# First MoE in five chunks of 480 or 384 tokens instead of eight of 288, with new due times for the list

## The chip, the cores and the metric

The kernel runs on one core of a Trainium2 chip. The metric is device time in microseconds of one execution, as the median of several runs; lower is better. The core has five engines that work through queues of their own, each in order: TensorE (PE) for matmuls, VectorE (DVE), ScalarE (ACT), GpSimd (POOL), and SyncE (SP), whose queue here issues all DMAs. Work on different engines is ordered by semaphores alone. SBUF is the on-chip memory, PSUM the eight banks that matmuls write.

## What is computed

```python
def _attn_ref(q, k, v):            # 4 batches, 8 heads, 576 tokens, 64 per head
    ...
    masks = np.stack([mask_plain if h < H // 2 else mask_dil for h in range(H)], axis=0)
    scores = np.where(masks[None, :, :, :], scores, -1000000000.0)
    ...
    return np.matmul(attn, v).astype(np.float32)

def _moe_ref(x, w1, w2, w3, w_out):    # 2304 tokens, 512 -> 1024 -> 512
    a = x @ w1
    b = x @ w2
    h = a * b @ w3
    return (h @ w_out).astype(np.float32)

def _moe2_ref(x, w_in, w_out, a, b):   # 2304 tokens, 512 -> 2048 -> 512
    h = x @ w_in
    ...
    g = P / (Q + 1e-06)
    return (g @ w_out).astype(np.float32)
```

Windowed attention (in half of the heads over every fourth token), then a first MoE block, then a second with a rational function in its middle. The weights arrive as float64.

## The kernel before

The kernel multiplies W3 by Wout once (`w3_mm`, W3o), so that the first MoE is two layers: x @ w1 and x @ w2 with their product (L1), then the product @ W3o (L2). Every operand of these layers is split into a high and a low part of type float32r, and a product is three matmuls: high by high, high by low, low by high. A weight slab arrives as 64-bit words and is turned into float32 by ACT and DVE: `scale` on ACT, then `shift`, `sign`, `low_bits` on DVE; or, for the slabs that the constants BY_ACT name, `top_bits` on ACT as well and only `ends` and `middle` on DVE. Then `high` on ACT and `low` on DVE split it.

Work comes in two stages. In the first (`phase1`, to 437.9 us) nothing is issued where it is written. All of it, attention by batch, pair of heads and half (G from 0 to 31), W3o, the 16 slabs of w1 and w2, both layers by chunk, and the preparation of the second MoE's 32 slabs that goes back to DRAM as `wd`, is given to a planner (`Plan`) as jobs with an engine, an estimated duration, predecessors, buffers and a due time. The planner plays the engines through and takes, on each engine, the ready job of the earliest due time; the instructions are then issued in the order of the starts that it found. That order is fixed from then on: on the chip an engine waits for the head of its queue. Due times come from the table T, which `main_jobs` fills in the order W3o, L1 and L2 of each chunk, and from constants (GAP, AHEAD, LEAD, B_FROM, PACE).

The tokens of the first MoE are cut into eight chunks of TA = 288, two for a batch of 576. `l1(k, m, e)` is a group of 12 matmuls into one of the two banks `ab`; ACT copies the first of a pair (`l1_copy`, tile a_sb), DVE multiplies it by the second (`l1_mul`, tile p), ACT and POOL split the product (`l1_high`, `l1_low`, tile pp). Chunk 0 and 1 run their first layers together, slab by slab; the products of chunk 1 are stored to DRAM and loaded again (`p_store`, `p_load`) since SBUF doesn't hold both. `l2(k, h, i)` accumulates the second layer in two banks for each half h, `acc` and then `ab` (in the last chunk `sc`); ACT and DVE split the result (x2, x2l) and SP stores it as `x2d`.

The attention output of a batch is one tile xs in pool xs01 (batches 0 and 2, on the right side of SBUF) or xs23 (1 and 3, on the left). The words of the second MoE's slabs go through two buffers in turn, w32 and w33. Each of these slabs is one turn: load, `scale`, three steps on DVE, store to `wd`, and the buffer is free for the next load.

The second stage (`phase2`) runs the second MoE over token blocks of 512 (the last of 256), with x loaded back from x2d as tiles XS0 to XS4 (XS0, XS1 and XS4 in pool b3 on the right, XS2 and XS3 in b1 on the left). It begins with one step, then runs L2 of the last chunk (`tail`) and goes on.

Of the kernel before, what the change touches and what calls it, by code (L numbers as in the profile page):

```python
# [26 lines left out]
TA = 288  # L27
NA = NT // TA
# [159 lines left out]
class Kern:  # L188
# [277 lines left out]
    def l1_copy(self, k, m):  # L466
        self.a_sb[k, m] = self.tp.tile([P, TA], F32, tag="t", bufs=5, name="a_sb")
        self.nc.scalar.copy(self.a_sb[k, m], self.ab[k, m, 0][:, 0:TA])

    def l1_mul(self, k, m):  # L470
        p = self.pp[k, m] = self.tp.tile([P, TA], F32, tag="t", bufs=5, name="p")
        self.nc.vector.tensor_tensor(out=p, in0=self.a_sb[k, m], in1=self.ab[k, m, 1][:, 0:TA],  # L472
                                     op=ALU.mult)

    def l1_high(self, k, m):
        p, e = self.pp[k, m], m % 2
        if e == 0:
            self.p2[k, m // 2] = self.gp.tile([P, 2, 2, TA], F32R, tag="g", bufs=5, name="pp")
        self.nc.scalar.copy(self.p2[k, m // 2][:, 0, e], p)  # L479
# [589 lines left out]
```

## Time and profile before

| what | us |
|---|---|
| median of 3 runs | 854.42 |
| lowest and highest run | 854.24, 855.56 |
| span of the profiled execution (first to last instruction) | 852.4 |
| first stage, to the first matmul of the second MoE (L848) | 437.9 |
| PE busy | 840.8 |
| DVE, ACT, POOL busy | 569.0, 546.2, 328.5 |

The page gives no time of its own for the profiled execution beside its span; the span stands 2.0 us under the median. Busy times say how long an engine had an instruction in work; for PE the ends of matmuls are modelled and neighbours overlap, so the distance of starts is the better measure. Lines such as L462 are lines of the kernel before; in the changed kernel the same work has other line numbers (L462 becomes L487, L513 becomes L522, L225 becomes L229).

### The profile page before, as it was taken

The numbers are of one execution on the slowest core, as the hardware profiler recorded it, in microseconds if no ns is written. First come the engines' busy times: TensorE is split into PE (matmuls) and PEld (weight loads), VectorE is DVE, ScalarE is ACT, GpSimd is POOL, SyncE is SP. The second block draws the span as 40 slices with busy tenths as digits, with TensorE's granted clock in tenths as the row PEclk, the third lists the DMA queues.
The fourth block names the chain that finished last, engine by engine and source line by source line (L and its number), as shares of the span: only waits on it lengthen the run. The fifth ranks groups of instructions, "written<-read, shape, count | busy, mean of one in ns | idle before, by whom it ended". The sixth has DMA issues, their size and how long they took to land.

```text
span 852.4 us, 14597 instructions
## 1 busy us (share of the span) xinstructions
PE 840.8 (99%) x5256; PEld 722.5 (85%) x5256; DVE 569.0 (67%) x1240; ACT 546.2 (64%) x1226; POOL 328.5 (39%) x305
## 2 busy tenths in 40 slices
PE   9999999999999999999999999999999999999998
PEld 5557789989999999999998788888888888888886
DVE  6999985777657223411226887788778777797775
ACT  7787677664466335622336977777777777777773
POOL 1330123223043212402124665565556655564443
PEclk9999999999999999999999999999999999999999
DMA  9986275875866212070343000010000100001112
GB/s 352 321 315 216 88 252 188 276 252 177 282 200 212 71 48 76 2 253 1 106 141 125 13 13 25 13 37 26 13 13 25 37 14 14 13 25 50 42 42 90
DMA packets 43464, 95.06 MB, mean 112 GB/s; under 512 B 4736, under 2 KB 13952, under 8 KB 43392
## 3 DMA queue, kind: packets, MB, share of 16 engines
q1 hardware_dynamic: 43392, 94.13, 32.6%
q8 instruction: 41, 0.67, 0.3%
q14 instruction: 31, 0.25, 0.1%
HBM read 71.57 MB, written 22.54 MB: 110 GB/s over the span
## 4 chain that ended last, share of the span: by engine, by line
PE 89%; ACT 5%; DMA 3%; DVE 2%; issue 0%; POOL 0%; SPq 0%; POOLq 0%; DVEq 0%; ACTq 0%
PE ab L462 24%; PE acc L898 11%; PE sc L898 11%; PE ab L848 11%; PE px L848 10%; PE acc L513 6%; PE ab L513 4%; PE sc L351 2%; PE acc L442 2%; PE px L409 2%; PE px L394 2%; PE ab L442 1%; ACT pr L375 1%; PE sc L442 1%; PE px L307 1%; PE sc L513 1%
## 5 line engine op out<-in xcount | busy, mean ns | idle before, releaser
L462 PE MATMUL ab<-xs,w 128*128 128x288 f32 x1536 | 215.9, 299 | 2.6 <-DVE x2l L526 2.2
L462 PEld LDWEIGHTS ab<-xs,w 128*128 128x128 f32 x1536 | 205.7, 188 | 8.4 <-DVE x2l L526 2.9
L859 POOL TENSOR_TENSOR y<-y,v 128x512 f32<-128x512 f32 x72 | 95.9, 1331 | 142.9 <-ACT y L858 142.6
L387 POOL TENSOR_TENSOR pr<-pr,sm 96x384 f32<-96x384 f32 x64 | 57.6, 919 | 173.3 <-DVE sm L382 98.4
L898 PE MATMUL acc<-w,gg 128*128 128x512 f32 x432 | 109.8, 391 | 1.5 <-ACT r L869 1.5
L898 PE MATMUL sc<-w,gg 128*128 128x512 f32 x432 | 109.4, 391 | 0.0
L483 POOL TENSOR_TENSOR pp<-p,pp 128x288 fp32r<-128x288 f32 x56 | 47.2, 843 | 158.5 <-ACT pp L479 158.4
L848 PE MATMUL ab<-XS,w 128*128 128x512 f32 (+1 forms) x480 | 105.4, 370 | 0.0
L848 PE MATMUL px<-XS,w 128*128 128x512 f32 (+1 forms) x480 | 105.3, 370 | 0.0
L885 POOL TENSOR_TENSOR gg<-t,gg 128x512 fp32r<-128x512 f32 x72 | 93.7, 1302 | 10.6 <-ACT gg L884 10.1
L848 PEld LDWEIGHTS px<-XS,w 128*128 128x128 f32 x480 | 83.9, 188 | 16.3
L848 PEld LDWEIGHTS ab<-XS,w 128*128 128x128 f32 x480 | 83.8, 188 | 16.2
L898 PEld LDWEIGHTS acc<-w,gg 128*128 128x128 f32 x432 | 80.8, 188 | 19.2 <-ACT r L869 1.9
L898 PEld LDWEIGHTS sc<-w,gg 128*128 128x128 f32 x432 | 80.9, 188 | 17.2
L472 DVE TENSOR_TENSOR p<-a_sb,ab 128x288 f32<-128x288 f32 x64 | 29.0, 453 | 85.3 <-PE ab L462 67.0
L375 ACT ACTIVATE pr<-pr,sm 96x128 f32<-96x128 f32 x192 | 74.7, 393 | 2.5 <-DVE sm L367 2.5
L876 DVE SCALAR_TENSOR_TENSOR v<-y,cs,r 128x512 f32<-128x512 f32 x72 | 71.3, 990 | 0.0
L868 ACT ACTIVATE r<-y,cs 128x512 f32<-128x512 f32 x72 | 52.3, 726 | 14.5 <-POOL y L859 14.4
L479 ACT CAST pp<-p 128x288 fp32r<-128x288 f32 x56 | 24.2, 432 | 56.5 <-DVE p L472 56.5
L858 ACT ACTIVATE y<-v,cs 128x512 f32<-128x512 f32 x72 | 58.8, 817 | 2.4
L225 ACT ACTIVATE dec<-words 128x512 f32<-128x512 f32 x72 | 47.5, 672 | 19.3 <-DMA words<-moe_w_in 8.4
L513 PE MATMUL acc<-pp,w 128*128 128x288 f32 x384 | 55.1, 298 | 0.0
(90 smaller groups left out, 1298.1 us busy)
## 6 DMA issues: line engine op xcount, KB each, us to landing
words<-moe_w SPq DMA_DIRECT2D x32, 512.0 KB, 6.2
words<-moe_w_out SPq DMA_DIRECT2D x24, 512.0 KB, 4.4
words<-moe_w_in SPq DMA_DIRECT2D x16, 512.0 KB, 4.4
wd<-dec SPq DMA_DIRECT2D x32, 256.0 KB, 2.3
c<-wd SPq DMA_DIRECT2D x32, 256.0 KB, 2.6
vb<-v SPq DMA_DIRECT2D x16, 384.0 KB, 4.2
XS<-x2d SPq DMA_DIRECT2D x6, 1024.0 KB, 6.9
kT<-k SPq DMA_DIRECT2D x16, 304.0 KB, 4.3
```

The source lines that it names most:

```text
L225: self.nc.scalar.activation(out=d.bitcast(F32), in_=s["words"].bitcast(F32)[:, :, 1], func=AF.Copy, scale=2.0 ** -112)
L375: self.nc.scalar.activation(out=pr[:, i], in_=pr[:, i], func=AF.Exp, scale=-1.0, bias=sm[:, 0, i:i + 1], accum_out=sm[:, 1, i:i + 1])
L387: self.nc.gpsimd.tensor_tensor(out=pr[:, i], in0=pr[:, i], op=ALU.mult, in1=sm[:, 2, i].unsqueeze(2).to_broadcast([QT, 3, P]))
L462: self.nc.tensor.matmul(t[:, 0:TA], w[:, s[0], c * P:(c + 1) * P], xs[:, s[1], c, tok], start=n == 0, stop=n == 11)
L513: self.nc.tensor.matmul(self.l2_acc[k, n][:, 0:TA], self.W3o[m][0][:, a, n * P:(n + 1) * P], self.p2[k, i][:, c, m % 2], start=m == 0 and ...
L848: nc.tensor.matmul(t[:, e * nt:(e + 1) * nt], w[:, s[0], c * P:(c + 1) * P], XS[blk][:, s[1], c], start=n == 0, stop=n == 11)
L858: nc.scalar.activation(out=w, in_=v, func=AF.Identity, scale=self.b1, bias=self.b0)
L859: nc.gpsimd.tensor_tensor(out=w, in0=w, in1=v, op=ALU.mult)
L868: nc.scalar.activation(out=r, in_=yy[i][1], func=AF.Ln, bias=self.c1)
L876: nc.vector.scalar_tensor_tensor(out=v, in0=w, scalar=self.c1, in1=r, op0=ALU.add, op1=ALU.mult)
L885: nc.gpsimd.tensor_tensor(out=t[:, 1], in0=u, in1=t[:, 0].bitcast(F32), op=ALU.subtract)
L898: nc.tensor.matmul(acc[g, blk][tk], t[:, s[0], j:j + P], w[:, s[1]], start=f + e == 0 and s == (0, 0), stop=f + e == FG - 1 and s == (1, 0))
```

## The change

The first MoE is cut into five chunks of 480, 480, 384, 480 and 480 tokens (CH) that cross the batches. Each chunk has an xs tile of its own, in three slots: chunks 0, 2 and 3 in pool xsa on the right, 1 and 4 in xsb on the left. The output of one half of a pair of heads may lie in two chunks and is then written in two pieces. Chunk 1 no longer runs with chunk 0: the list's order is W3o in full, then L1 and L2 chunk by chunk; all products stay in SBUF (tile g: eight buffers of 2 x 512), and the DRAM tile pd with its stores and loads is gone. The W3 slabs rotate through five buffers instead of six, the second MoE's slabs all through w32. Four W3 slabs and eight of w1 and w2 are done by ACT's top_bits instead of eight and sixteen. Due times (GAP0, GAP, AHEAD0, AHEAD, PACE, W3_AT) and the planner's durations are set anew.

```diff
-TA = 288
-NA = NT // TA
+CH = ((0, 480), (480, 480), (960, 384), (1344, 480), (1824, 480))
+NA = len(CH)
+TM = max(n for _, n in CH)
+NR = 3
+HS = S // 2
...
-TL = NT - TA - BLK[NB - 2][0]
+TL = CH[-1][0] - BLK[NB - 2][0]
...
-W12SLOT = ("p0", "p1", "p2", "p3", "w34", "w35", "w30", "w31",
+NW3 = 5
+W12SLOT = ("p0", "p1", "p2", "p3", "w33", "w34", "w30", "w31",
...
-GAP0, GAP = 4.0, 7.0
+GAP0, GAP = 3.0, 9.0
...
-W3_AT = 4
-PACE = 1.15
-
-BY_ACT3 = 8
-BY_ACT1, BY_ACT2 = 0, 16
+AHEAD0, AHEAD = 14.0, 16.0
+W3_AT = 8
+PACE = 1.25
+
+BY_ACT3 = 4
+BY_ACT1, BY_ACT2 = 0, 8
...
     def att_high(self, G):
-        b = G // (2 * HP)
-        if b not in self.xs:
-            pool = (self.xs01, self.xs23)[b % 2]
-            self.xs[b] = pool.tile([P, 2, KC, S], F32R, tag="xs", bufs=1, name="xs")
-        dst, src = self.att_x(G)
-        self.nc.scalar.copy(dst[:, 0], src)
+        for c in self.fresh.get(G, ()):
+            pool = (self.xsa, self.xsb, self.xsa)[c % NR]
+            self.xs[c] = pool.tile([P, 2, KC, CH[c][1]], F32R, tag=f"xs{c % NR}", bufs=1, name="xs")
+        for dst, src in self.att_x(G):
+            self.nc.scalar.copy(dst[:, 0], src)
 
     def att_low(self, G):
-        dst, src = self.att_x(G)
-        self.nc.vector.tensor_tensor(out=dst[:, 1], in0=src, in1=dst[:, 0].bitcast(F32),
-                                     op=ALU.subtract)
+        for dst, src in self.att_x(G):
+            self.nc.vector.tensor_tensor(out=dst[:, 1], in0=src, in1=dst[:, 0].bitcast(F32),
+                                         op=ALU.subtract)
...
     def l1(self, k, m, e):
-        xs, w, tok = self.xs[k // 2], self.w12[2 * m + e]["w"], slice(k % 2 * TA, (k % 2 + 1) * TA)
+        xs, w, nt = self.xs[k], self.w12[2 * m + e]["w"], CH[k][1]
...
-                self.nc.tensor.matmul(t[:, 0:TA], w[:, s[0], c * P:(c + 1) * P], xs[:, s[1], c, tok],
+                self.nc.tensor.matmul(t[:, 0:nt], w[:, s[0], c * P:(c + 1) * P], xs[:, s[1], c],
...
-    def p_store(self, m):
-        self.nc.sync.dma_start(out=self.pd[m // 2, :, m % 2], in_=self.pp[1, m])
-
-    def p_load(self, i):
-        w = self.p2[1, i] = self.gp.tile([P, 2, 2, TA], F32R, tag="g", bufs=5, name="pp")
-        self.nc.sync.dma_start(out=w[:, 1].bitcast(F32), in_=self.pd[i])
...
-                self.l2_acc[k, n] = self.bank(L2BANKS[k == NA - 1][h])
+                self.l2_acc[k, n] = self.bank(L2BANKS[k >= NA - 2][h])
...
-            s, wb, db, fn, a = words(src, Q, f"w3{n % 6}", n < BY_ACT3)
+            s, wb, db, fn, a = words(src, Q, f"w3{n % NW3}", n < BY_ACT3)
...
-        for m in range(M1):
-            for k in range(2):
-                l1_jobs(k, m)
-        l2_jobs(0)
-        back_jobs()
-        l2_jobs(1)
-        for k in range(2, NA):
+        for k in range(NA):
             for m in range(M1):
                 l1_jobs(k, m)
             if k < NA - 1:
...
-            s, wb, db, fn, a = words(src, Q, f"w3{2 + i % 2}")
+            s, wb, db, fn, a = words(src, Q, "w32")
```

How the order on the engines moves is shown at three places.

PE, from the end of the W3 products to the first layer of chunk 0 (acc, sc: W3 products; ab<-xs,w: first layer). Before:

```order
L409 MATMUL px<-pT,vb 64x96 x6
L442 MATMUL sc<-x 128x512 x2
L462 MATMUL ab<-xs,w 128x288 x96
L442 MATMUL acc<-x 128x512 x2
L442 MATMUL sc<-x 128x512 x2
L442 MATMUL acc<-x 128x512 x2
L442 MATMUL sc<-x 128x512 x2
L462 MATMUL ab<-xs,w 128x288 x12
L442 MATMUL acc<-x 128x512 x2
L462 MATMUL ab<-xs,w 128x288 x84
L442 MATMUL sc<-x 128x512 x2
L462 MATMUL ab<-xs,w 128x288 x24
```

In the changed kernel:

```order
L413 MATMUL px<-pT,vb 64x96 x6
L467 MATMUL sc<-x 128x512 x2
L467 MATMUL acc<-x 128x512 x2
L467 MATMUL sc<-x 128x512 x2
L487 MATMUL ab<-xs,w 128x480 x24
L355 MATMUL sc<-kT,qT 96x128 x6
L487 MATMUL ab<-xs,w 128x480 x12
```

Six groups of W3 products that stood among the first layers of chunks 0 and 1 now stand ahead of chunk 0, and attention of batch 1 (sc<-kT,qT) begins after two groups of its first layer.

PE, from the last piece of attention to the last chunk's first layer (acc, ab or sc<-pp,w: second layer). Before:

```order
L409 MATMUL px<-pT,vb 64x96 x6
L513 MATMUL ab<-pp,w 128x288 x48
L462 MATMUL ab<-xs,w 128x288 x192
L513 MATMUL acc<-pp,w 128x288 x48
L513 MATMUL ab<-pp,w 128x288 x48
L462 MATMUL ab<-xs,w 128x288 x192
```

In the changed kernel:

```order
L413 MATMUL px<-pT,vb 64x96 x6
L522 MATMUL ab<-pp,w 128x384 x48
L487 MATMUL ab<-xs,w 128x480 x192
L522 MATMUL acc<-pp,w 128x480 x48
L522 MATMUL sc<-pp,w 128x480 x48
```

The sequence is the same, with wider matmuls, and the last second layer of the list ends in sc instead of ab.

ACT, from the evictions of one second layer into the next chunk's first layer (a_sb<-ab: `l1_copy`; pp<-p: `l1_high`; dec<-words: `scale` of a slab of the second MoE). Before, chunks 5 and 6:

```order
L522 CAST x_4720<-ab 128x288
L522 CAST x_4723<-ab 128x288
L468 COPY a_sb<-ab 128x288
L479 CAST pp<-p 128x288
L468 COPY a_sb<-ab 128x288
```

In the changed kernel, chunks 2 and 3:

```order
L532 CAST x_3518<-ab 128x384
L532 CAST x_3539<-ab 128x384
L229 ACTIVATE dec<-words 128x512
L494 COPY a_sb<-ab 128x480
L504 CAST pp<-p 128x480
L494 COPY a_sb<-ab 128x480
L229 ACTIVATE dec<-words 128x512
L504 CAST pp<-p 128x480
```

Slabs of the second MoE, which were all done by then, now stand between the copies of the first layer to the end of the list.

## Rows read from the trace of the kernel before

**Rows 1.** The page: engines' busy time (its part 1); clock granted in 40 slices.

```profile
PE 840.8 (99%) x5256; PEld 722.5 (85%) x5256; DVE 569.0 (67%) x1240; ACT 546.2 (64%) x1226; POOL 328.5 (39%) x305
...
PEclk9999999999999999999999999999999999999999
```

**Rows 2.** The page: shares of the chain that ended last, by engine.

```profile
PE 89%; ACT 5%; DMA 3%; DVE 2%; issue 0%; POOL 0%; SPq 0%; POOLq 0%; DVEq 0%; ACTq 0%
```

**Rows 3.** PE in order of time, list stage: start us, length us, engine, line, operation, count.

```profile
74.50 13.36 PE L462 MATMUL ab<-xs,w 128*128 128x288 f32 x96
87.69 1.88 PE L442 MATMUL acc<-x 128*128 128x512 f32 x4
89.41 1.88 PE L442 MATMUL sc<-x 128*128 128x512 f32 x4
...
188.64 23.96 PE L462 MATMUL ab<-xs,w 128*128 128x288 f32 x180
212.44 4.95 PE L513 MATMUL acc<-pp,w 128*128 128x288 f32 x36
...
217.67 1.84 PE L513 MATMUL acc<-pp,w 128*128 128x288 f32 x12
219.44 0.72 PE L409 MATMUL px<-pT,vb 128*64 128x96 f32 x12
...
282.81 24.27 PE L462 MATMUL ab<-xs,w 128*128 128x288 f32 x180
306.92 1.34 PE L513 MATMUL acc<-pp,w 128*128 128x288 f32 x9
```

**Rows 4.** What PE waited for: us in total, times, longest.

```profile
PE ab L462 <- DVE x2l L526: 2.2, 3, 1.7
...
PE acc L442 <- DVE x L264: 1.0, 1, 1.0
```

**Rows 5.** PE in order of time, last stage, 512-wide matmuls of token blocks 0 to 3.

```profile
456.27 5.76 PE L848 MATMUL px<-XS,w 128*128 128x512 f32 x24
461.87 2.96 PE L848 MATMUL ab<-XS,w 128*128 128x512 f32 x12
...
491.29 2.88 PE L848 MATMUL ab<-XS,w 128*128 128x512 f32 x12
494.01 1.52 PE L898 MATMUL acc<-w,gg 128*128 128x512 f32 x6
```

**Rows 6.** Groups by line and form: slab preparation on DVE (busy us, mean ns | idle).

```profile
L233 DVE SCALAR_TENSOR_TENSOR dec<-words,dec 128x512 int32<-128x512 int32 x48 | 35.0, 735 | 0.8
...
L248 DVE SCALAR_TENSOR_TENSOR dec<-words,dec 128x512 int32<-128x512 int32 x32 | 24.7, 774 | 0.8
...
L229 DVE TENSOR_SCALAR dec<-dec 128x512 int32<-128x512 int32 x48 | 23.6, 497 | 16.0 <-ACT dec L225 15.9
...
L260 DVE SCALAR_TENSOR_TENSOR words<-words 128x512 int32<-128x512 int32 x24 | 17.6, 738 | 6.2 <-ACT words L255 6.2
...
L264 DVE SCALAR_TENSOR_TENSOR dec<-dec,words 128x512 int32<-128x512 int32 x16 | 11.5, 725 | 0.2
```

**Rows 7.** Busy time of the engines from 74.50 to 148.50, of instructions (x).

```profile
74.50:148.50 74.00, 73.65 (x561) 64.97 (x559) 59.76 (x161) 51.59 (x144) 16.13 (x18) 1.00 0.52 172
```

**Rows 8.** DVE in order of time: the first low part of a w1/w2 slab.

```profile
64.48 0.69 DVE L274 TENSOR_TENSOR w<-dec,w 128x512 fp32r<-128x512 f32 x1
```

**Rows 9.** SP, ACT and DVE in order of time: turns of one words slot.

```profile
200.20 0.38 SPq L211 DMA_DIRECT2D words<-moe_w_in  x1
...
207.39 0.38 SPq L211 DMA_DIRECT2D words<-moe_w_in  x1
...
215.51 0.39 SPq L211 DMA_DIRECT2D words<-moe_w_in  x1
...
203.79 0.67 ACT L225 ACTIVATE dec<-words 128x512 f32<-128x512 f32 x1 [1.76 <-DMA words<-moe_w_in]
...
206.25 0.69 DVE L248 SCALAR_TENSOR_TENSOR dec<-words,dec 128x512 int32<-128x512 int32 x1
```

More of the change, by code (lines that the diff above doesn't have):

```diff
@@ new lines, in att_x @@
+        parts = []
+        for c, (at, n) in enumerate(CH):
+            if hp < HP // 2:
+                t0 = b * S + half * HS
+                lo, hi = max(at, t0), min(at + n, t0 + HS)
+                if lo < hi:
+                    parts.append((self.xs[c][:, :, hp, lo - at:hi - at], r[:, lo - t0:hi - t0]))
+            else:
+                lo, hi = max(at, b * S), min(at + n, (b + 1) * S)
+                if lo < hi:
+                    dst = self.xs[c][:, :, hp, lo - at:hi - at].rearrange("p w (i r) -> p w r i", r=4)
+                    src = r.rearrange("p (r i) -> p r i", r=2)[:, :, (lo - b * S) // 4:(hi - b * S) // 4]
+                    parts.append((dst[:, :, 2 * half:2 * half + 2], src))
@@ new lines, in att_x, with chunks, touched @@
+        return parts
+    @staticmethod
+    def chunks(b):
+        return [c for c, (at, n) in enumerate(CH) if at < (b + 1) * S and at + n > b * S]
+    def touched(self, G):
+        u, half = divmod(G, 2)
+        b, hp = divmod(u, HP)
+        t0, n = (b * S + half * HS, HS) if hp < HP // 2 else (b * S, S)
+        return [c for c, (at, m) in enumerate(CH) if at < t0 + n and at + m > t0]
+    def att_high(self, G):
+        for c in self.fresh.get(G, ()):
[3 more added lines that the diff above has]
+            self.nc.scalar.copy(dst[:, 0], src)
@@ L466, in l1_copy @@
     def l1_copy(self, k, m):
[L467 to L468 removed]
+        nt = CH[k][1]
+        self.a_sb[k, m] = self.tp.tile([P, nt], F32, tag="t", bufs=5, name="a_sb")
+        self.nc.scalar.copy(self.a_sb[k, m], self.ab[k, m, 0][:, 0:nt])
     def l1_mul(self, k, m):
[L471 to L472 removed]
+        nt = CH[k][1]
@@ L473, in l1_mul @@
+        p = self.pp[k, m] = self.tp.tile([P, nt], F32, tag="t", bufs=5, name="p")
+        self.nc.vector.tensor_tensor(out=p, in0=self.a_sb[k, m], in1=self.ab[k, m, 1][:, 0:nt],
                                      op=ALU.mult)
     def l1_high(self, k, m):
[L476 to L479, printed above, removed]
+        w = self.p2[k, m] = self.gp.tile([P, 2, TB], F32R, tag="g", bufs=8, name="pp")
@@ L565, in phase1 @@
             T[job] = t
[L566 removed]
+            t += 1.72 if job[0] == "w3" else mm12(job[1]) * PACE
         end = t
@@ L599, in phase1 @@
             pv = done[G] = add("PE", 0.78, self.att_pv, G, after=pc + [lv], new=px[2:], use=[pTb, lb[2]])
-            first = G % (2 * HP) == 0
-            hi = add("ACT", 0.43, self.att_high, G, after=[pv] + ([low[G - 1, "h"]] if not first else []),
-                     new=[xsb[b]] if first else [], use=px[2:] + ([] if first else [xsb[b]]))
+            hi = add("ACT", 0.25 + 0.22 * len(xb), self.att_high, G, after=[pv] + ([low[G - 1, "h"]] if G else []),
+                     new=[xsb[c] for c in fresh], use=px[2:] + [b for b in xb if b not in [xsb[c] for c in fresh]])
             low[G, "h"] = hi
-            low[G] = add("DVE", 0.5, self.att_low, G, after=[hi], use=px[2:] + [xsb[b]], due=due)
+            low[G] = add("DVE", 0.3 + 0.25 * len(xb), self.att_low, G, after=[hi], use=px[2:] + xb, due=due)
         self.nd = 0
@@ L705, in back_jobs @@
-        def back_jobs():
-            pl, gbs = parts.setdefault(1, ([], []))
-            for i in range(M1 // 2):
-                gb = buf("g")
-                d = T["l2", 1, 0, i] - 8
-                a = add("SP", 0.95, self.p_load, i, new=[gb], due=d,
-                        after=[kept[2 * i], kept[2 * i + 1]] + parts[0][0][-1:])
-                a = add("ACT", 0.67, self.p_high, i, after=[a], use=[gb])
-                pl += [add("DVE", 0.72, self.p_low, i, after=[a], use=[gb], port=True)] * 2
-                gbs.append(gb)
+            pl, gbs = parts.setdefault(k, ([], []))
@@ L716, in l2_jobs @@
+            gbs.append(buf("g"))
+            hi = add("ACT", act(k) + 0.02, self.l1_high, k, m, after=[mu], new=gbs[-1:], use=[tb[1]], due=d + 5)
+            pl.append(add("POOL", 0.08 + 0.0024 * CH[k][1], self.l1_low, k, m, after=[hi], use=[tb[1], gbs[-1]]))
         def l2_jobs(k):
@@ L991, in run @@
             over = ExitStack()
-            self.xs01 = over.enter_context(self.pool("xs01", side="right"))
+            self.xsa = over.enter_context(self.pool("xsa", side="right"))
             self.at = over.enter_context(self.pool("at", side="right"))
```

117 lines of the change are left out of this document (54 added, 63 removed).

## The prediction

> **What bounds the kernel now.** Four views, in this order. The page first: TensorE (PE) is busy for 99% of the span and its granted clock is full in every slice, 2.4 GHz throughout [rows 1]. A busy PE alone proves little, since the ends of matmuls are modelled. The second view is therefore the chain of work that ended last: 89% of it is PE, ACT has 5%, DMA 3%, DVE 2% [rows 2]. The third is PE in order of time, where the distance from one start to the next is the true price of a matmul, whatever the modelled ends say: a stretch of 180 first-layer matmuls begins at 188.64 and the next work at 212.44 [rows 3], and nothing stands between. The fourth lists what PE waited for in the list's stage: 2.2 us for banks that the second layer had not yet given back, 1.0 us for W3 slabs at the start [rows 4], little else. So PE sets the time nearly everywhere; what the change takes from PE comes off the end, unless another engine becomes late.
>
> **The price of a matmul by its width.** 288 columns: (212.44 − 188.64) / 180 = 132.2 ns in one chunk, (306.92 − 282.81) / 180 = 133.9 in another [rows 3]; I use 133. 512 columns have two prices in the last stage: 24 of them from 456.27 to 461.87 give 233.3 ns (token blocks 0 and 1), 12 from 491.29 to 494.01 give 226.7 (blocks 2 and 3) [rows 5]. At 2.4 GHz 288 columns last 120.0 ns and 512 last 213.3, so a matmul pays 13 ns beyond its columns, or 20 in the dearer place.
>
> **Fewer, wider matmuls.** Eight chunks of 288 need 8 x (192 + 96) = 2304 matmuls in the two layers; five chunks need 5 x 288 = 1440, of which 1152 are 480 wide and 288 are 384 wide. PE's total falls from 5256 to 4392. Before: 2304 x 133 = 306.4 us. No row is 480 or 384 wide, so both ends come from the rows on either side. On the line from 133 at 288 to 226.7 at 512 (0.418 ns a column) a 480 costs 213.3 and a 384 costs 173.2: 245.7 + 49.9 = 295.6 us, **-10.8**. On the line to 233.3 (0.448) they cost 219.0 and 176.0: 252.3 + 50.7 = 303.0, **-3.4**. Which holds where? The dear blocks 0 and 1 lie in the pool b3 on the right side of SBUF, the cheap 2 and 3 in b1 on the left; and of the two stretches of 288 the dearer one (133.9) reads a right-hand tile, the other a left-hand one. In the changed kernel the attention output of chunks 0, 2 and 3 lies on the right; that of chunks 1 and 4 and the second layer's operand lie on the left. With place deciding: 384 x 219.0 + 192 x 176.0 + 768 x 213.3 + 96 x 173.2 = 84.1 + 33.8 + 163.8 + 16.6 = 298.3 us, **-8.1**, which I take.
>
> **Boundaries between chunks.** The second layer's second half uses the two ab banks that the next chunk's first layer wants; PE waited 2.2 us for them in three places [rows 4]. Such boundaries fall from six to three (the last second layer inside the list now uses sc), but each eviction is two thirds wider. Ends -2.2 and +0.5; I take -1.0.
>
> **Switches to attention.** Twelve second-layer matmuls alone between attention pieces take 219.44 − 217.67 = 1.77 us [rows 3] where 12 x 133 is 1.60: some 0.09 us for each change. The list has 152 changes between attention and other matmuls before and 146 after: -0.5 (ends -0.5 and 0).
>
> **The first 20 us.** Four of the first eight W3 slabs move from ACT's top_bits to DVE's three steps: shift, sign and low_bits at 0.49 + 0.73 + 0.77 in place of ends and middle at 0.73 + 0.72 (busy over count, [rows 6]), 0.54 more each, 2.2 us on DVE. PE already waits there 1.0 us for DVE's x [rows 4]; on the other side attention's first products now stand later in PE's list and leave room for W3. Ends 0 and +2.2; I take +0.6.
>
> **Edits at no cost.** The store of chunk 1's product to DRAM, its load and second split go: eight stores, four loads, four splits on ACT and on DVE, none of which PE's waits name. Attention's output is split in 56 pieces on ACT and on DVE where there were 32, and POOL's low parts get longer; these engines are at 64%, 67% and 39% of the span [rows 1]. With that cover gone 24 pieces more on DVE would cost 24 x 0.49, the shortest group of [rows 6], 12 us at the very most.
>
> **Sum.** -8.1 - 1.0 - 0.5 + 0.6 = -9.0 us; ends -13.5 and -0.7. The profiled execution spans 852.4 us and the median of the runs is 854.42, so 2.0 us lie around the span; I expect a span of 843.4 and a time of **845.4 us**.
>
> **Rival 1: the excess goes with the columns, not with the matmul.** If every wide matmul pays the dear price, the widths bring 3.4 and the rest 0.9: 850.1 us. For it: half of the 512-wide matmuls do cost 233.3 [rows 5], and their excess of 20 ns over 13 at 288 is in the ratio of the widths. Against it: the other blocks run the same code at 226.7 with 13 ns of excess, as at 288. Chance 0.12.
>
> The Trainium skill, page "TensorE: Matmul & The Clock Gate", section "Back-to-back issue gap", puts a warm matmul at its columns over 2.4 GHz plus a fixed 2.5 ns. By that figure the 864 matmuls that go would bring only 864 x 2.5 = 2.2 us, and with the other terms the time would be 851.3. The rows do not agree: 288 columns cost 13 ns more than 120.0.
>
> **Rival 2: DVE is late for chunk 0.** Before, the sixteen w1/w2 slabs are used by chunks 0 and 1 together; now each serves one chunk of 480 at first. From 74.50 to 148.50 DVE was busy 59.8 of 74.0 us [rows 7]. PE's 384 matmuls of 133 in that stretch (51.1) become 192 of 213 (40.9), 10.2 less, and six W3 groups of 89.41 − 87.69 = 1.72 [rows 3], 10.3 us, move ahead of it: 53.5 us of PE are left. DVE gets eight slabs from ACT, 8 x 0.54: 64.1 us. It lacks 10.6, against a lead of 74.50 − 64.48 = 10.0 between the first low part [rows 8] and PE's first use of it [rows 3]. The W3 groups that moved ahead lengthen PE's run before, and so that lead; this speaks against. Half the lead lost is 5 us: 850.4 us; all of it 856. Chance 0.10.
>
> **Rival 3, the slower side: the one slot w32 sets the pace.** The 32 slabs of the second MoE go through one words buffer instead of two, spread to the end of the list. A turn is load, scale on ACT, three steps on DVE, store, next load; ACT's scale now stands between the first layer's copies, so a late load holds up the copy behind it, and then PE's two ab banks. In the rows a turn goes so: load issued at 200.20, scale at 203.79, low bits from 206.25, the slot's next load at 207.39: 7.2 us; the following one takes 8.1, to 215.51, with another slot's slab in between [rows 9]. In the changed list eleven turns lie between the start of chunk 3's first layer and the tenth group of chunk 4's: 192 + 96 + 108 matmuls of 213, 84.5 us, 7.7 a turn. At 7.2 the chain fits; at 8.1 it costs 11 x 0.42 = 4.6 us and the time is 850; from 7.7 + 9.0 / 11 = 8.5 on the kernel is slower than before, and at 9.0 it loses 14.5, for 860 us. The x2d stores and the loads of XS0 and XS1 in the same queue speak for long turns; DVE and ACT, which have little else in that stretch, against. Chance 0.09 of a result above 856.
>
> That the change doesn't do what it says can be left out: the widths stand in the list of instructions.
>
> **How the numbers follow.** Forecast (841 to 849): 0.64; below that 0.02. Rival 1: 0.12. Rival 2: 0.10, of which 0.03 lands within 0.2% of before. Rival 3 slower: 0.09. That several small waits just eat the gain: 0.03. A measurement of this kernel can tell about 0.2%, 1.7 us, from no change, so faster means below 852.7: 0.64 + 0.02 + 0.12 + 0.07 = 0.85; same 0.06; slower 0.09. The range 840.5 to 852.5 holds the forecast, rival 1, most of rival 2 and a turn of 8.1; it leaves out 0.17.
>
> **What would show it.** PE's count is 4392. The distance of two 480-wide starts is 213 ns on the left and 219 on the right; 219 everywhere is rival 1, 213 everywhere is 2.7 us more gain. If rival 2 holds, PE's waits name DVE's low part of w (L274 before) ahead of chunk 0. If rival 3 holds, ACT's scale waits for words in chunks 3 and 4, and PE for ACT's a_sb. The last stage keeps its length. A new wait of PE over 4 us in the first 160 us, or waits of more than 4 us in all in chunks 3 and 4, would make the forecast wrong.

## The result and the profile after

| kernel | median us | lowest to highest | ratio to before, 95% interval |
|---|---|---|---|
| before | 854.66 | 854.24 to 855.56 | |
| changed | 844.37 | 843.66 to 845.82 | 0.9881, 0.9862 to 0.9900 |
| forecast | 845.4 | 840.5 to 852.5 | 0.9892 |

The changed kernel is 10.3 us faster. Its profiled execution spans 841.9 us against 852.4, so 10.5 us are to be found in the trace. The page first, its part 1 and the chain's shares by engine, to be read beside [rows 1] and [rows 2]:

```profile
PE 833.6 (99%) x4392; PEld 677.3 (80%) x4392; DVE 578.6 (69%) x1236; ACT 533.9 (63%) x1182; POOL 331.8 (39%) x289
...
PE 92%; DVE 3%; ACT 2%; DMA 1%; issue 0%; POOL 0%; DVEq 0%; POOLq 0%; ACTq 0%
```

The count is the forecast 4392, and PE sets the time even more than before: 92% of the chain where it was 89%. What PE waited for, the counterpart of [rows 4] (us in total, times, longest):

```profile
PE acc L897 <- ACT r L868: 1.5, 1, 1.5
PE px L311 <- POOL ident L291: 1.4, 1, 1.4
PE sc L355 <- DVE sm L371: 0.8, 1, 0.8
PE acc L467 <- DVE x L268: 0.4, 1, 0.4
PE ab L487 <- DVE x2l L537: 0.2, 1, 0.2
PE px L398 <- POOL pr L391: 0.2, 1, 0.2
```

The wait for x2l at the boundaries between chunks fell from 2.2 to 0.2 us, that for W3 slabs from 1.0 to 0.4. No line names ACT's a_sb or a slab of w1 and w2. And PE in order of time (start, length, line, count), from the last second layer of chunk 2 into the last stage, the counterpart of [rows 3] and [rows 5]:

```profile
314.62 42.18 PE L487 MATMUL ab<-xs,w 128*128 128x480 f32 x192 [0.19 <-DVE x2l L537]
356.63 10.56 PE L522 MATMUL acc<-pp,w 128*128 128x480 f32 x48
367.03 10.56 PE L522 MATMUL sc<-pp,w 128*128 128x480 f32 x48
377.43 41.77 PE L487 MATMUL ab<-xs,w 128*128 128x480 f32 x192
419.04 2.97 PE L847 MATMUL ab<-XS,w 128*128 128x512 f32 x12
421.85 10.58 PE L522 MATMUL acc<-pp,w 128*128 128x480 f32 x48
...
445.46 5.76 PE L847 MATMUL px<-XS,w 128*128 128x512 f32 x24
451.06 2.96 PE L847 MATMUL ab<-XS,w 128*128 128x512 f32 x12
453.86 1.55 PE L897 MATMUL acc<-w,gg 128*128 128x512 f32 x6
```

From start to start: chunk 3, whose operand lies on the right, (356.63 - 314.62) / 192 = 218.8 ns a matmul; chunk 4, on the left, (419.04 - 377.43) / 192 = 216.7; the second layer (377.43 - 367.03) / 48 = 216.7. The last stage begins at 419.04 in place of 437.92; it is 8.4 us longer because the second layer inside it is that of 480 tokens and no longer of 288.

### The profile page after: what moved, and what is told of

Same layout as the page of the kernel before. It is cut to its first block, busy times and chain, and to the rows that moved or that the text cites. A ratio compares the mean times of both kernels' runs of the same rounds, so it can differ in the third digit from the quotient of the medians.

```text
span 841.9 us, 12683 instructions
## 1 busy us (share of the span) xinstructions
PE 833.6 (99%) x4392; PEld 677.3 (80%) x4392; DVE 578.6 (69%) x1236; ACT 533.9 (63%) x1182; POOL 331.8 (39%) x289
## 4 chain that ended last, share of the span: by engine, by line
PE 92%; DVE 3%; ACT 2%; DMA 1%; issue 0%; POOL 0%; DVEq 0%; POOLq 0%; ACTq 0%
PE ab L487 24%; PE acc L897 11%; PE sc L897 11%; PE ab L847 11%; PE px L847 10%; PE acc L522 6%; PE ab L522 3%; PE sc L355 3%; PE acc L467 3%; PE sc L522 2%; PE px L413 2%; PE px L398 2%; PE sc L467 2%; PE ab L467 1%; DMA words<-moe_w 1%; DVE v L875 1%
## 5 line engine op out<-in xcount | busy, mean ns | idle before, releaser
L487 PE MATMUL ab<-xs,w 128*128 128x480 f32 (+1 forms) x960 | 211.5, 375 | 0.2 <-DVE x2l L537 0.2
L487 PEld LDWEIGHTS ab<-xs,w 128*128 128x128 f32 x960 | 174.8, 188 | 25.1 <-DVE x2l L537 0.5
L508 POOL TENSOR_TENSOR pp<-p,pp 128x480 fp32r<-128x480 f32 (+1 forms) x40 | 50.4, 1260 | 158.6 <-ACT pp L504 152.4
L884 POOL TENSOR_TENSOR gg<-t,gg 128x512 fp32r<-128x512 f32 x72 | 93.7, 1301 | 10.7 <-ACT gg L883 10.1
L499 DVE TENSOR_TENSOR p<-a_sb,ab 128x480 f32<-128x480 f32 (+1 forms) x40 | 25.3, 634 | 53.6 <-PE ab L487 34.6
L233 DVE TENSOR_SCALAR dec<-dec 128x512 int32<-128x512 int32 x60 | 31.6, 527 | 38.4 <-ACT dec L229 38.3
L504 ACT CAST pp<-p 128x480 fp32r<-128x480 f32 (+1 forms) x40 | 23.2, 580 | 51.5 <-DVE p L499 51.1
## 6 DMA issues: line engine op xcount, KB each, us to landing
kT<-k SPq DMA_DIRECT2D x16, 304.0 KB, 3.8
```

Source lines behind the costliest of these rows:

```text
L487: self.nc.tensor.matmul(t[:, 0:nt], w[:, s[0], c * P:(c + 1) * P], xs[:, s[1], c], start=n == 0, stop=n == 11)
L884: nc.gpsimd.tensor_tensor(out=t[:, 1], in0=u, in1=t[:, 0].bitcast(F32), op=ALU.subtract)
```

## Experiments: is it the width, or the due times?

Each ratio below compares a run with the kernel before on the same chip, where that kernel's median was 854.1 to 854.9; the change alone stood at 844.37.

**Width undone.**

```diff
-CH = ((0, 480), (480, 480), (960, 384), (1344, 480), (1824, 480))
+CH = ((0, 288), (288, 288), (576, 288), (864, 288), ..., (2016, 288))
-NR = 3
+NR = 4
...
-            due = T["l1", self.chunks(b)[0] if b == 0 else b, 0, 0] - ...
+            due = T["l1", self.chunks(b)[0], 0, 0] - ...
```

The last two lines make the attention of a batch due ahead of the first chunk that it touches; the changed kernel takes the chunk that has the batch's number. With five chunks, of 480 or of 512 columns, both are the same chunk; here and with six chunks they are not.

> The changed kernel with its chunks cut back to eight of 288 tokens (four slots for the attention output, two on each side); everything else of the change stays: one chunk after the other, products in SBUF, new due times, slabs as changed. Theory A (my prediction: the gain is the matmuls that go): 2304 matmuls at the 133 ns of the rows are 306 us against the 300.3 us that the starts of the changed kernel add up to (384 x 218.2 + 384 x 216.5 + 384 x 216.7 + 192 x 174.2 + 96 x 174.0), so 5.7 us longer by that alone, and 1 to 3 us more for three more boundaries: 850 to 853 us, with 5256 matmuls on TensorE again. Theory B (the gain comes from the new due times and the order, width is nothing): 845 us or less.

Measured: 860.88 us, ratio 1.0063 (1.0042 to 1.0084); slower than before, and 16.5 us slower than the changed kernel, twice what theory A allowed. The price of the matmuls gives 5.7 of it, as expected: the matmuls of chunk 7 still cost 133 ns each. Of the rest, PE shows 2.9 us in the first chunk:

```profile
112.65 1.32 PE L487 MATMUL ab<-xs,w 128*128 128x288 f32 x8 [0.33 <-ACT w L274]
114.59 0.80 PE L487 MATMUL ab<-xs,w 128*128 128x288 f32 x4 [0.62 <-DVE w L278]
115.84 1.33 PE L487 MATMUL ab<-xs,w 128*128 128x288 f32 x8 [0.45 <-ACT w L274]
118.63 0.81 PE L487 MATMUL ab<-xs,w 128*128 128x288 f32 x4 [1.47 <-DVE w L278]
```

PE waits here for slabs of w1 and w2 that are not split yet: rival 2, in a kernel that I had not priced it for. The busy time of the engines in the first layer of chunk 0, here and then in the changed kernel (stretch, its length, then PE, PEld, DVE, ACT, POOL, the granted clock, DMA):

```profile
83.70:124.90 41.20, 37.54 (x297) 33.82 (x296) 39.11 (x119) 29.68 (x98) 12.16 (x13) 0.96 0.20 66
```

```profile
82.90:140.30 57.40, 57.40 (x386) 46.38 (x384) 49.58 (x161) 41.47 (x141) 21.21 (x21) 1.00 0.27 86
```

DVE is busy for 39.1 of 41.2 us with 288 columns and 49.6 of 57.4 with 480. The sixteen slabs serve one chunk at a time now; a chunk of 480 gives the engines that prepare them 16 us more. All listed waits ahead of the last stage are 8.7 us against 3.0. So the 16.5 us have 5.7 in matmuls and 5.7 in waits. Another 1.7 is the clock: right behind the waits shown the granted clock was 0.66 from 120.0 to 125.0, and 5.0 x 0.34 = 1.7. Some 3.4 us I can't put to a line. That the waits come from the width alone is not shown: this kernel keeps the due times set for five chunks, which cost 7.5 us on the eight chunks of before (see below), and eight chunks in the one-chunk order with due times of their own were not run.

**Old due times on the new chunks.**

```diff
-GAP0, GAP = 3.0, 9.0
+GAP0, GAP = 4.0, 7.0
-AHEAD0, AHEAD = 14.0, 16.0
-W3_AT = 8
-PACE = 1.25
+AHEAD0, AHEAD = 1.0, 8.0
+W3_AT = 4
+PACE = 1.15
```

> The changed kernel with the due times of before (GAP0, GAP = 4, 7; AHEAD0, AHEAD = 1, 8; W3_AT = 4; PACE = 1.15); chunks, buffers and slabs stay as changed. The width's part stays the same (starts of the two layers: 300.3 us in the changed kernel against 306 before). Theory A (the waits that vanished between before and after, 7.8 to 4.5 us in the list of waits, vanished because chunks are longer and fewer): 844 to 846 us. Theory B (they vanished because the due times were set anew for this order): the waits come back, W3 and attention again in each other's way and the second layer's banks late, 3 to 6 us: 847 to 851 us.

Measured: 854.51 us, ratio 0.9999 (0.9983 to 1.0014). The whole gain is gone, more than theory B had. The rows below are from an execution of 857.93 us. The old due times of the start alone:

```diff
-GAP0, GAP = 3.0, 9.0
+GAP0, GAP = 4.0, 9.0
-AHEAD0, AHEAD = 14.0, 16.0
-W3_AT = 8
+AHEAD0, AHEAD = 1.0, 16.0
+W3_AT = 4
```

> The changed kernel with the old due times of the start alone (GAP0 = 4, AHEAD0 = 1, W3_AT = 4); GAP, AHEAD and PACE as changed. With all old due times the first first-layer matmul came at 92.61 in place of 82.94 and the end of the third second layer at 328.3 in place of 314.1. Theory A (the start loses it: attention of batch 0 is due one us before chunk 0 and ends too late, PE waits for pT and for W3 slabs): first layer from 90 us or later, 851 to 854 us. Theory B (the lists of the later batches, GAP, AHEAD and PACE, lose it): 844 to 847 us.

Measured: 853.64 us, ratio 0.9984 (0.9971 to 0.9997): 9.3 of the 10.1 us are lost at the start. PE in order of time there, in the run with all old due times; the entry in brackets is the idle time before and what ended it:

```profile
74.89 2.39 PE L467 MATMUL acc<-x 128*128 128x512 f32 x4 [1.89 <-DVE x L252]
...
91.46 1.22 PE L413 MATMUL px<-pT,vb 128*64 128x96 f32 x10 [3.75 <-ACT pT L404]
92.61 7.63 PE L487 MATMUL ab<-xs,w 128*128 128x480 f32 x25
```

The changed kernel starts its first layer at 82.94:

```profile
81.62 1.88 PE L467 MATMUL sc<-x 128*128 128x512 f32 x4
82.94 5.79 PE L487 MATMUL ab<-xs,w 128*128 128x480 f32 x24
```

With attention of batch 0 due 1 us ahead of chunk 0, W3 is used up before the last pieces of attention come: PE stands 3.75 us for pT with nothing else to do, since chunk 0 needs all of batch 0. With AHEAD0 = 14 those pieces lie among the W3 products, which fill PE meanwhile. The wait then costs more than its length, for the clock:

```profile
87.60:91.40 3.80, 0.11 (x2) 0.00 (x0) 2.85 (x5) 3.54 (x7) 0.00 (x0) 0.81 0.77 270
91.40:94.00 2.60, 2.54 (x14) 2.11 (x15) 2.60 (x6) 2.34 (x7) 0.00 (x0) 0.50 0.14 30
94.00:96.00 2.00, 2.00 (x7) 1.66 (x6) 2.00 (x5) 0.80 (x2) 0.00 (x0) 0.50 0.49 171
96.00:98.00 2.00, 2.00 (x9) 1.71 (x8) 1.97 (x5) 0.85 (x3) 0.00 (x0) 0.80 0.00 0
98.00:100.00 2.00, 2.00 (x11) 1.73 (x10) 1.53 (x3) 1.15 (x2) 0.00 (x0) 1.00 0.00 0
```

These are windows of the same run; the number before the last two is the granted clock. It is 0.81 over the wait, 0.50 (1.2 GHz) behind it and back at 1.00 from 98 on; the first 25 matmuls last 7.6 us where 25 x 217 ns is 5.4, so the wait took 2.2 us more. The wait of 1.89 us for a W3 slab, in the first line shown, was followed in the same way: 0.56 from 77.0 to 80.1, where four W3 matmuls take 3.21 us and otherwise 1.88. The Trainium skill, page "TensorE: Matmul & The Clock Gate", section "HAM oscillation — how this bites in real kernels", describes a wait of this kind that puts the engine back to half rate, so that the next burst starts slow; the trace agrees, with 0.50 from 91.4 to 96.0.

**The new due times alone, on the kernel before.**

```diff
-GAP0, GAP = 4.0, 7.0
+GAP0, GAP = 3.0, 9.0
-AHEAD = 8.0
-W3_AT = 4
-PACE = 1.15
+AHEAD0, AHEAD = 14.0, 16.0
+W3_AT = 8
+PACE = 1.25
...
```

> The kernel before, with the new due times alone (GAP0, GAP = 3, 9; AHEAD0, AHEAD = 14, 16; W3_AT = 8; PACE = 1.25); eight chunks, buffers and slabs as before. The changed kernel with the old due times lost 10 us, of which 9.7 us stood before its first first-layer matmul (92.61 against 82.94). Theory A (the new due times are a gain of their own): PE's waits before phase 2 fall from 6.3 us towards 3, so 851 to 852 us. Theory B (they only fit the new order, they mend what the single chunk at a time breaks): 854 us or slower.

Measured: 862.28 us, ratio 1.0087 (1.0057 to 1.0116). Theory B: they are a loss of 7.5 us on eight chunks. PE's waits grow, above all

```profile
PE ab L462 <- DVE x2l L526: 4.4, 4, 2.3
PE sc L351 <- DVE sm L367: 2.0, 5, 0.9
```

against 2.2 in [rows 4] for the first and none for the second. All listed waits ahead of the last stage are 9.9 us against 6.3, and behind the longest, of 2.29 us, the granted clock was 0.61 from 184 to 188: 4.0 x 0.39 = 1.6 us more. Which of the constants does it was not tried. So the two halves of the change do not add:

| median us | old due times | new due times |
|---|---|---|
| kernel before, eight chunks | 854.7 | 862.3 |
| changed kernel, five chunks | 854.5 | 844.4 |

The two rows differ in more than the count of chunks: the one-chunk order, the buffers, the slabs and the planner's durations changed with it. Of these only the slabs were tried by themselves, and the eight chunks in the one-chunk order above.

**Six chunks of 384.** The slots are turned by two, so that the last chunk lies on the left.

```diff
-CH = ((0, 480), (480, 480), (960, 384), (1344, 480), (1824, 480))
+CH = ((0, 384), (384, 384), (768, 384), (1152, 384), (1536, 384), (1920, 384))
...
-                    xsb[c] = buf(f"xs{c % NR}")
+                    xsb[c] = buf(f"xs{(c + 2) % NR}")
...
```

> Six chunks of 384 tokens (slots of the attention output turned by two, so that the last chunk lies on the left), all else as changed: 1728 matmuls of the two layers in place of 1440. Theory A (a fixed cost of 13 ns for each matmul): 288 x 13 = 3.7 us longer, 848 us, and more for one more boundary. Theory B (the rows of the changed kernel: 384 columns cost 174.0 to 174.2 and 480 cost 216.5 to 218.2, so the excess at 480 is 16.5 to 18 and at 384 is 14): 1728 x 174.1 = 300.8 us against 300.3, 0.5 us longer: 844.9 us, 845 to 846 with the boundary.

Measured: 858.59 us, ratio 1.0048 (1.0031 to 1.0065). Both theories fell on the time. On the price theory B is the nearer: 192 first-layer matmuls from 406.91 to 440.19 are 173.3 ns each, and 1728 such are 299.5 us, where B had 300.8 and A, which gave the 480 of the changed kernel an excess of 13 ns as well, 304.0. About half of what was lost is at the boundaries:

```profile
353.86 3.92 PE L487 MATMUL ab<-xs,w 128*128 128x384 f32 x12 [3.08 <-DVE x2l L537]
358.34 32.06 PE L487 MATMUL ab<-xs,w 128*128 128x384 f32 x180 [0.57 <-ACT a_sb L494]
```

x2l costs 5.1 us in two places, and after the longer wait twelve matmuls take 3.9 us where 2.1 would do, at a granted clock of 0.57 from 353.8 to 356.0. The due times were not set for six chunks, which I take for the reason but did not test; a price per matmul can't be read from such a run's total, only from its undisturbed stretches.

## Experiments: the slabs

**Slabs by ACT as before.**

```diff
-BY_ACT3 = 4
-BY_ACT1, BY_ACT2 = 0, 8
+BY_ACT3 = 8
+BY_ACT1, BY_ACT2 = 0, 16
```

> The changed kernel with eight W3 slabs and all sixteen w1 and w2 slabs by top_bits on ACT, as before the change. Theory A (my prediction's step: four W3 slabs moved to DVE cost 0.6 us at the start, the rest is hidden): 843.5 to 844.5 us, with PE's wait for the slabs of W3 not longer than the 0.4 us of the changed kernel. Theory B (ACT was the engine that was late, and the move to DVE was worth something): ACT has some 12 x 0.7 = 8 us more work in the first 140 us, pT and pr come later, PE waits 1 to 5 us more: 845.5 to 849 us.

Measured: 845.60 us, ratio 0.9891 (0.9876 to 0.9906). This is the lower edge of theory B, but the interval overlaps that of the change: moving twelve slabs to DVE is worth some 1 us, or nothing. PE's waits for W3 slabs are 0.5 us without the move and 0.4 with it, so the 0.6 us that I charged the move is not seen.

**A longer turn of w32.** The words of the last twelve slabs of the second MoE are loaded twice.

```diff
-        self.nc.sync.dma_start(out=words.rearrange("p a b -> p (a b)"), in_=s["src"])
+        for _ in range(2 if s.get("twice") else 1):
+            self.nc.sync.dma_start(out=words.rearrange("p a b -> p (a b)"), in_=s["src"])
...
+            s["twice"] = i >= 20
```

> The changed kernel with the words of the last twelve slabs of the second MoE loaded twice into w32, which makes a turn of this slot longer by a load of 3 us or so. In the changed kernel the eleven turns from 321.04 to 408.98 take 8.0 us on average and 6.5 to 6.7 at the shortest, and PE waits for none of them. Theory A (the prediction's rival 3: from 7.7 us a turn on every turn is paid in full): 11 x (11.0 - 8.0) = 33 us, 877 us. Theory B (the turns of 8 us hold slack, since the slot waits for ACT's place in the list; only what goes beyond 8.0 from the shortest turn of 6.6 counts): 11 x (6.6 + 3.0 - 8.0) = 18 us, 862 us. Theory C (the order hides it, the slot sets no pace): 844 to 846 us.

Measured: 883.12 us, ratio 1.0336 (1.0313 to 1.0359); 38.7 us slower than the change. In the changed kernel the DMA queue shows the turns (start of the load of words, the twelfth from the end and the last):

```profile
313.78 0.38 SPq L215 DMA_DIRECT2D words<-moe_w_in  x1
...
402.30 0.37 SPq L215 DMA_DIRECT2D words<-moe_w_out  x1
```

Eleven turns in 88.5 us, 8.0 each, and PE waits for none. With the second load, for the same slabs:

```profile
314.85 3.80 SPq L216 DMA_DIRECT2D words<-moe_w_in  x2
...
437.72 3.98 SPq L216 DMA_DIRECT2D words<-moe_w_out  x2
```

Eleven turns in 122.9 us, 11.2 each, as long as theory A had them, and now PE does what rival 3 said, it waits for ACT's copies, which stand behind `scale`, which stands behind the load:

```profile
PE ab L488 <- ACT a_sb L495: 20.5, 7, 4.9
PE ab L488 <- DVE p L500: 5.7, 2, 4.2
```

The turns are 11 x (11.2 - 8.0) = 35 us longer. Of these PE shows 26.2 as waits, and the clock takes more, a mean of 0.92 from 314.90 to 458.00 with stretches at 0.50 in it (345.0 to 349.0 the first):

```profile
314.90:458.00 143.10, 116.75 (x482) 96.42 (x483) 38.64 (x59) 28.57 (x51) 19.67 (x15) 0.92 0.51 168
```

Half the time of 143.1 x (1 - 0.92) / 0.5 = 22.9 us at half clock would be some 11 us lost; with the waits that is 37 of the 38.4 us by which this stretch is longer. Rival 3 was a true mechanism; where between 8.0 and 11.2 us a turn becomes dear was not tried. A turn of 8 us has slack in it: in the changed kernel `scale` follows its load by 3.5 to 4.2 us where ACT waits for the words, but by up to 7.3 (373.89 to 381.15) where ACT comes to it later.

## Experiments: what a matmul costs

**Chunks of 512 and 256.**

```diff
-CH = ((0, 480), (480, 480), (960, 384), (1344, 480), (1824, 480))
+CH = ((0, 512), (512, 512), (1024, 256), (1280, 512), (1792, 512))
...
```

> Five chunks of 512, 512, 256, 512 and 512 tokens in place of 480, 480, 384, 480, 480; same count of matmuls, same total of columns. Theory A (a fixed cost for a matmul, 13 ns, and 20 where the operand lies on the right at 512 columns): first layers of chunks 0 and 3 at 233.4, the other 512-wide ones at 226.7, 256 at 116.7 as in token block 4: 384 x 233.4 + 768 x 226.7 + 288 x 116.7 = 297.3 us against 300.3, so 3 us faster than the changed kernel: 841.4 us. Theory B (the excess goes with the columns, 216.5 for 480 means 231 for 512 and 115 for 256): 1152 x 231 + 288 x 115 = 299.2, 1 us, no change that can be measured: 843.3 us. If copies and products of 512 columns come too late for the banks, PE shows waits for ACT or DVE and it is slower than 845.

Measured: 844.62 us, ratio 0.9883 (0.9864 to 0.9903), as the change. The prices are those of theory A:

```profile
310.66 45.06 PE L487 MATMUL ab<-xs,w 128*128 128x512 f32 x192 [0.28 <-DVE x2l L537]
355.56 11.08 PE L522 MATMUL acc<-pp,w 128*128 128x512 f32 x48
...
377.36 43.68 PE L487 MATMUL ab<-xs,w 128*128 128x512 f32 x192
420.88 2.97 PE L847 MATMUL ab<-XS,w 128*128 128x512 f32 x12
```

233.9 ns on the right (chunk 3), 226.7 on the left (chunk 4). But x2l costs 2.1 us at two boundaries of the profiled execution, which took 846.5, and pr and sm 2.0 in all, 2.9 more than in the changed kernel, which ate the 3.0 that theory A had.

**The right side moved by 32 bytes; everything moved to multiples of 128 bytes.** A pool of one tile at the right edge moves all behind it; in the second kernel it is 96 bytes, and a constant tile on the left grows by 64.

```diff
+            edge = right.enter_context(self.pool("edge", side="right"))
+            self.nc.vector.memset(edge.tile([P, 8], F32, name="pad"), 0.0)
```

> The changed kernel with everything on the right side of SBUF moved down by 32 bytes (a pool of one tile of 32 bytes at the edge). In the program's addresses the left tiles xs of chunks 1 and 4, XS2 and XS3 start at a multiple of 64 bytes, the right ones 32 bytes behind one; after the move all start at a multiple of 64. Theory A (the address decides the dear price, not the side): 512-wide matmuls of XS0 and XS1 fall from 233.4 to 226.7, 384 x 6.7 = 2.6 us; the first layer of chunks 0 and 3 from 218.2 to 216.5, 384 x 1.7 = 0.7 us: 841.1 us. Theory B (the side decides, as my prediction had it): no change, 844.4 us, XS0 and XS1 stay at 233.4.

> The changed kernel with the right side moved down by 96 bytes and the left side up by 64, so that weights and moving operands all start at a multiple of 128 bytes (before: 64 bytes behind one on the left, 96 on the right). Theory A (only where a row stands within 64 bytes counts): as e3, 841.1 us, left-hand 512-wide matmuls stay at 226.7. Theory C (128 bytes count): left-hand matmuls become cheaper too; their whole excess over the columns at 2.4 GHz is 13.3 ns at 512 columns, so at most some 13 ns for each of 3700 wide matmuls, 48 us; at a third of that 828 us.

Measured: 842.88 us, ratio 0.9858 (0.9842 to 0.9874), and 844.34, 0.9871 (0.9850 to 0.9892). In the first, PE in the last stage, token blocks 0 and then 1:

```profile
446.37 5.60 PE L847 MATMUL px<-XS,w 128*128 128x512 f32 x24
451.81 2.88 PE L847 MATMUL ab<-XS,w 128*128 128x512 f32 x12
454.53 1.52 PE L897 MATMUL acc<-w,gg 128*128 128x512 f32 x6
```

(454.53 - 451.81) / 12 = 226.7 where the changed kernel has (453.86 - 451.06) / 12 = 233.3. So it is not the side of SBUF that decides; my prediction had the right price for the wrong reason. Only half of the 3.3 us came, by medians whose intervals overlap, since the 256-wide matmuls of block 4 rose from 116.8 to 119.7 ns (0.6 us) and the list ended 1.1 us later (420.13 against 419.04) with small waits. The second kernel refutes theory A too: its addresses are multiples of 128 on both sides, and yet blocks 0 and 1 cost 233.1. A candidate that is left is the distance between the moving operand and the weights, since the weights were moved as well. A third kernel puts unused tiles of a bytes ahead of the x tiles and z behind them:

```diff
+            PADS = {0: (0, 128), 1: (0, 32), 4: (0, 64), 3: (96, 0), 2: (64, 0)}
...
+                    a, z = PADS[n]
+                    if a:
+                        self.nc.vector.memset(pool.tile([P, a // 4], F32, name=f"pa{n}"), 0.0)
                     self.XS[n] = pool.tile([P, 2, KC, BLK[n][1]], F32R, name=f"XS{n}")
+                    if z:
+                        self.nc.vector.memset(pool.tile([P, z // 4], F32, name=f"pz{n}"), 0.0)
```

> The changed kernel with small unused tiles between the x tiles of the last stage, so that each stands at another distance from the weights modulo 256 bytes: XS0 64, XS1 192, XS2 160, XS3 96, XS4 224 (in the changed kernel 32, 32, 0, 0, 32). The runs so far show for 512 columns 226.7 ns at distance 0 (left, and right when moved by 32 bytes), 233.3 at 32, 232.9 at 128; for 256 columns 120.0 at 0, 116.7 at 32, 119.9 at 128. Theory A (only distance 0 is cheap for 512): XS0 to XS3 all near 233, 2 x 192 x 6.6 = 2.5 us longer, 846.9 us. Theory B (a multiple of 64 bytes in the address itself is cheap, as in e3): XS0 and XS1 fall to 226.7 (addresses 184064 and 200576, multiples of 64), XS2 and XS3 (multiples of 32 alone) rise to 233.3: no change, 844.4 us. Theory C (no rule of either kind): some distance gives less than 226.7 and shows what is to be had.

Measured: 848.19 us, ratio 0.9908 (0.9885 to 0.9931), 3.8 us slower than the changed kernel. Mean time from start to start inside groups of equal matmuls in the last stage, over the changed kernel and these three, by the distance of x from the weights modulo 256 bytes (addresses of the program):

| distance | 0 | 32 | 64 | 96 | 128 | 160 | 192 | 224 |
|---|---|---|---|---|---|---|---|---|
| 512 columns, ns | 226.7 | 233.5 | 230.1 | 234.3 | 233.1 | 233.5 | 233.3 | |
| 256 columns, ns | 119.7 | 116.8 | | | 119.7 | | | 118.2 |

Distance 0 is best for 512 columns, as theory A of that run had it, but for 64, and at 256 columns 0 and 128 are the worst tried. At 512 columns the address itself does not decide: block 0 at a multiple of 256 cost 230.1 with weights 192 behind one, block 2 at a multiple of 256 cost 226.7 with weights at a multiple of 256 too (the second kernel). None of the seven tried gives less than 226.7, so 13.3 ns of excess stay at each of them. Only distance 0 was seen at more than one pair of addresses. At 480 columns the distance alone does not decide either: at distance 128 the first layer of chunk 4 costs 217.7 in the changed kernel and 213.2 in the second, where weights and operand have both moved by 64. Why it is so, the runs don't say.

**All together.** Chunks of 512 and 256, due times set for them, 32 bytes between the tiles on the right so that wide operands lie at distance 0 and 256-wide ones at 32.

```diff
-CH = ((0, 480), (480, 480), (960, 384), (1344, 480), (1824, 480))
+CH = ((0, 512), (512, 512), (1024, 256), (1280, 512), (1792, 512))
-GAP0, GAP = 3.0, 9.0
-LEAD = 20.0
-AHEAD0, AHEAD = 14.0, 16.0
-PACE = 1.25
-BY_ACT3 = 4
-B_FROM = 120.0
+GAP0, GAP = 4.25, 8.5
+LEAD = 30.0
+AHEAD0, AHEAD = 12.0, 23.0
+PACE = 1.2
+BY_ACT3 = 0
+B_FROM = 130.0
...
+            if c == 0:
+                self.nc.vector.memset(pool.tile([P, 8], F32, name="pad"), 0.0)
...
+                    if n == 1:
+                        self.nc.vector.memset(pool.tile([P, 8], F32, name="pad"), 0.0)
...
```

> Chunks of 512, 512, 256, 512 and 512 tokens as in e2, the due times set for them (GAP0, GAP = 4.25, 8.5; LEAD = 30; AHEAD0, AHEAD = 12, 23; PACE = 1.2; B_FROM = 130; no W3 slab by top_bits), and unused 32-byte tiles that put the 512-wide operands on the right (xs of chunks 0 and 3, XS0, XS1) at distance 0 from the weights modulo 256 bytes and leave the 256-wide ones (xs of chunk 2, XS4) at 32. Theory A (the prices by width and distance, and the waits that due times set, add up): from e2's 844.6 us the first layers of chunks 0 and 3 give 384 x (233.2 - 227.3) = 2.3 us, XS0 and XS1 384 x (233.3 - 226.7) = 2.5 us, and of e2's 4.1 us of waits for x2l, sm and pr 1 to 3 us go: 837 to 839 us. Theory B (widths of 512 make ACT, DVE and POOL late whatever the due times, as in e2): the places alone, 839.8 us or more.

Measured: 837.43 us, ratio 0.9803 (0.9789 to 0.9816), 6.9 us faster than the changed kernel, theory A.

```profile
305.95 43.81 PE L489 MATMUL ab<-xs,w 128*128 128x512 f32 x192 [0.28 <-DVE x2l L539]
349.60 11.04 PE L524 MATMUL acc<-pp,w 128*128 128x512 f32 x48
...
371.36 43.68 PE L489 MATMUL ab<-xs,w 128*128 128x512 f32 x192
414.88 2.88 PE L849 MATMUL ab<-XS,w 128*128 128x512 f32 x12
```

227.3 ns in chunk 3 and 226.7 in chunk 4, and the wait for x2l is 0.3 us in all where it was 2.1. How much of the 6.9 us is the places and how much the due times and the W3 slabs was not separated; theory A had 4.8 for the places.

## Why the prediction was right, and where it was not

The time was forecast within 1.0 us. That matmuls on PE set the time, and that fewer and wider ones take less of it, was right. The terms of the sum stand less well.

| term | forecast us | in the trace us |
|---|---|---|
| widths | -8.1 | -5.7 |
| boundaries | -1.0 | -2.0 (x2l 2.2 to 0.2) |
| switches to attention | -0.5 | 152 to 146 changes, as forecast; not to be told from the rest |
| first 20 us | +0.6 | -0.6 (wait for W3 slabs 1.0 to 0.4) |
| waits for pT, xs, a_sb against sm, pr | not in the sum | -0.7 (1.7 gone, 1.0 new) |
| last stage apart from the second layer in it | 0 | +0.3 |
| rest | | -1.8 |
| span | -9.0 | -10.5 |

That the total came so near is partly luck: the widths gave 2.4 us less than forecast and all else together 3.9 more. And the sign "the last stage keeps its length" holds only without the second layer in it; with it the stage is 8.4 us longer.

- **Widths: the mechanism right, the size off.** By the mean of starts, 480 columns cost 216.5 (chunks 1, 4), 218.2 (chunks 0, 3) and 216.7 ns (second layer), 384 cost 174.2 and 174.0: 300.3 us against 306.0 before. I drew a line from 288 to 512 and put 213.3 for 480 on the left. The excess over the columns is not a line: 13 at 288, 14 at 384 (13.3 with six chunks), 16.5 at 480 and 13.3 again at 512. 768 matmuls at 3.4 ns too little are the 2.6 us that failed. The dear price on the right, 219.0 forecast, is 218.2; the side is not its reason.
- **Rival 1 is out.** The excess is not in ratio to the columns: 256 pay 10 to 13 ns, 480 pay 16.5 to 18.2, 512 pay 13.3 to 21. (The 20 and 13 ns that spoke for it stand as 1.5 to 1, the widths 512 and 288 as 1.8 to 1.) The fixed 2.5 ns of the Trainium skill, page "TensorE: Matmul & The Clock Gate", section "Back-to-back issue gap", which that section gives for a single matmul by itself and not for a stream of weight loads and matmuls, agrees with none of them.
- **Rival 2** did not come in the changed kernel, and came when the chunks were cut to 288 under the same due times. I had reckoned 64.1 us of DVE against 53.5 of PE in chunk 0; the trace has 49.6 against 57.4. More attention of batch 1 stands among the first-layer groups and makes the stretch longer; above all DVE had done more ahead of it, busy for 75.0 of the first 82.9 us where it was 62.6 of 74.5 before.
- **Rival 3** was named with the right chain of waits, ACT's copies behind `scale` behind the load. Its point (dear from 7.7 us a turn on) was too early: 8.0 cost nothing, 11.2 cost 38.7 us.
- **Edits at no cost: the step that failed as reasoning.** I gave the new due times no price of their own. They are worth 10.1 us on five chunks and cost 7.5 on eight. The forecast came out because it compared the two programs as they are, with the order already in the rows; as a statement of what brings the gain ("fewer, wider matmuls") it was half the story. Five chunks without the new due times bring nothing (854.5).

## What to carry to other kernels

Where a list is planned by due times, a change of tile size and the due times are one change: measured apart, each half here was worth nothing or less, together 10 us. Price a matmul from starts in an undisturbed stretch at the width that will run, and if there is none, keep both neighbours as bounds and not a line between them. Larger chunks also help the engines that prepare weights, since each slab then covers more time: 57.4 us for sixteen slabs here, in place of 41.2.

## What the runs showed of the hardware that I had not expected

- The time of a float32r matmul from start to start changes with the places of the moving operand and the weights in SBUF: 226.7 to 234.3 ns at 512 columns, 116.8 to 119.7 at 256. For x in the last stage at 512 columns it was 226.7 wherever the two lay at distance 0 modulo 256 bytes, while at 256 columns distance 0 was no better than any other tried. An unused tile of 32 bytes was worth 2.5 us of the last stage.
- Waits of 3.75, 4.08 and 4.94 us on TensorE (all old due times; those of the start; the double load) were followed by stretches with a granted clock of 0.50, 1.2 GHz, though work was there again. In the first of them 3.75 us of wait cost 6.0. The length of a wait alone does not tell whether this comes: 1.89 us was followed by 0.56 with all old due times and 1.90 us by the full clock with those of the start, 3.08 us by 0.57 with six chunks and 2.81 us by the full clock with the double load.
